# Query sketch of the first chunk in eight 32x64 matmuls, two v pieces on GpSimd's queue, larger weight loads

## The chip, the cores and the metric

The kernel runs on one core of one Trainium2 chip. The metric is the device time of one execution in microseconds (us), as a median of several runs. A core has five engines with instruction queues of their own: TensorE (PE in the profile, with PEld for its weight loads), VectorE (DVE), ScalarE (ACT), GpSimd (POOL) and SyncE (SP). Sixteen DMA engines move data; transfers are issued from SP's, ACT's or GpSimd's queue.

## What is computed

Polysketch attention over 4 batches, 4 heads, 1088 positions and head width 32, then a feed-forward layer with squared ReLU of width 2048, all in float32:

```python
def phi(x):
    a = np.einsum('rd,bhsd->bhsr', S1, x)      # r = 8
    b = np.einsum('rd,bhsd->bhsr', S2, x)
    return np.einsum('bhsi,bhsj->bhsij', a, b).reshape(*x.shape[:-1], 64)
q_p, k_p = phi(q), phi(k)
kv = np.einsum('bhsf,bhsd->bhfd', k_p, v)
z = np.sum(k_p, axis=2)
num = np.einsum('bhsf,bhfd->bhsd', q_p, kv)
den = np.einsum('bhsf,bhf->bhs', q_p, z)[..., None] + 1e-06
x = (num / den).transpose(0, 2, 1, 3).reshape(4352, 128)
h = np.maximum(x @ w_in, 0.0)                  # w_in 128 x 2048
out = (h * h) @ w_out                          # w_out 2048 x 128
```

## The kernel before

The 4352 tokens of x are cut into ten chunks of the feed-forward layer (256, 384, 448, 448, five of 512, 256 tokens). For each chunk PE multiplies by the 16 blocks of w_in (`ffn1`, L597, result in PSUM tile `pg`), ACT and DVE take the ReLU (`relu`, L607 and L609, tile `gt`) and the square (`square`, L620 and L622, tile `g`), and PE adds up the 16 blocks of w_out (`ffn2`, L641 and L636, tile `po`). A planner, the class `_Order`, lays the attention of later chunks and batches between these matmuls by costs and due times; it begins after the prologue and its inputs are not touched by the change.

The prologue (L221 to L847) is written out by hand, and its order of program text is the order on each engine. It makes x for the first 256 tokens:

- Loads (L221 to L229): S1 and S2; k of batch 0 in two pieces (columns 0 to 512, then the rest); the first 256 columns of q; v in eight pieces, four partition groups p of 32 rows by the ranges 0 to 4 and 4 to 9 of the nine k tiles. Piece (p = 0, 0 to 4) is issued from ACT's queue, all others from SP's.
- `keep_warm` gives PE bf16 matmuls of constants (L692), W0 = 5 ahead of the small matmul L703 that spreads S1 and S2 (tile `sp`, copied to `ss` by ACT at L706), and W1 = 3 after it.
- From L707 SP issues the rest: a second part of q, w_in in four pieces of 512 columns (256 KB each), w_out in four pieces of 256 KB, and the third part of q. The loads of the next batches follow on the same queue.
- `a_kT0` (DVE, L290) transposes k into `kt`; `a_qT` (DVE, L296) transposes q into `qT`.
- `a_kf` (L315) sketches k: for each tile of 128 positions, four matmuls with 32 stationary columns. ACT copies the second factor to `kb` (L321); `a_kp0` (DVE, L331) multiplies the factors into `kp`.
- `q0` (L756) sketches the first 256 columns of q into the four-bank PSUM tile `x0`. Its stationary operand `sq` holds S1's or S2's rows for two heads, with zeros where the heads do not match; GpSimd makes it from `ss` and the mask `own_q` (L721). ACT copies one factor to `qb0` (L767), and DVE multiplies the two into `qp0` (L774).
- `a_kv0` (L396) adds up kp times v and kp's sums over the nine tiles into `kvp`; its first matmul contracts all 128 partitions of v.
- The denominators (L816), the numerators (L821) and a few small steps give xT for the first 256 tokens (L844). `cast_wi` (GpSimd, L685) casts w_in in four pieces from `w_in32`. A matmul at L835 reads the first of them, and then `ffn1` begins.

PSUM tiles `pg` and `po` have two buffers each, `att` (four banks) has one.

Of the kernel before, what the change touches and what calls it, by code (L numbers as in the profile page):

```python
# [14 lines left out]
def _ap(t: bass.AP, p0: int, np_: int, off: int, free):  # L15
    p = list(t.ap)[0]
    return bass.AP(
        t.tensor, t.offset + p0 * p[0] + off, [[p[0], np_]] + [list(d) for d in free]
    )
# [88 lines left out]
def kernel(  # L108
# [11 lines left out]
    nc = tc.nc  # L120

    B, H, S, D = 4, 4, 1088, 32
# [5 lines left out]
    GT, G2, LA = 4, 6, 3.5  # L128
    LU = 4
    KC = [(0, 160), (160, 128)]  # L130
    W0, W1, W3 = 5, 3, 1
    ND, QT, WI, KL, QL = 2, 6.0, (1.0, 1.9), (30.0, 8.0), 4.0


# [10 lines left out]
    mult = mybir.AluOpType.mult  # L145
# [10 lines left out]
    psf = ctx.enter_context(tc.tile_pool(name="psf", bufs=2, space=bass.MemoryType.PSUM))  # L156
# [3 lines left out]
    def sb(name, cols, dt=F32, rows=128):  # L160
        return cpool.tile([rows, cols], dt, tag=name, name=name)
# [7 lines left out]
    kT, qT = sb("kT", SP), sb("qT", SP)  # L169
    xT = sb("xT", B * S + SP - S, F32R)  # L170
    w_in32, w_o, w_in = sb("w_in32", 2048), sb("w_o", 2048), sb("w_in", 2048, F32R)
    s_nat, ss, s2f = sb("s_nat", 32, rows=16), sb("ss", 80), sb("s2f", 32)
# [24 lines left out]
    def load_v(eng, b, p, t0=0, t1=NT):  # L197
        n = 32 * ((t1 if p < 3 else min(t1, NT - 2)) - t0)
        eng.dma_start(
            _ap(vn[b % 2], 32 * p, 32, 32 * t0, [[32 * NT, H], [1, n]]),  # L200
            bass.AP(
                v.tensor, v.offset + b * H * S * D + 32 * first(b, t0, p),
                [[G * D, 32], [S * D, H], [1, n]],
            ),
        )

    def load_wi(eng, c):
        eng.dma_start(
            w_in32[:, 512 * c : 512 * c + 512], moe_w_in[:, 512 * c : 512 * c + 512]
        )  # L210

    def load_wo(eng, c):
        eng.dma_start(
            _ap(w_o, 0, 128, 512 * c, [[128, 4], [1, 128]]),
            bass.AP(
                moe_w_out.tensor, moe_w_out.offset + c * 512 * 128,
                [[128, 128], [128 * 128, 4], [1, 128]],
            ),
        )

# [1 line left out]
    nc.sync.dma_start(s_nat[8:16, :], S2[:, :])  # L222
    load_k(nc.sync, 0, 0, 512)
    load_k(nc.sync, 0, 512, S)
    load_v(nc.scalar, 0, 0, 0, 4)
    load_q(nc.sync, 0, 0, 256)
    for t0, t1 in ((0, 4), (4, NT)):
        for p in range(0 if t0 else 1, 4):
            load_v(nc.sync, 0, p, t0, t1)  # L229

    zero_a = sb("zero_a", 8)
    nc.scalar.copy(zero_a[:, :], nc.const_aps.tensor(0.0, (128, 8), F32))

    sq, sel = sb("sq", 256), sb("sel", 320, rows=16)
    nc.vector.memset(sel[:, :], 0.0)
    nc.gpsimd.memset(_ap(vn[0], 96, 32, 32 * (NT - 2), [[32 * NT, H], [1, 64]]), 0.0)
    nc.gpsimd.memset(vn[0][:, VC : VC + 32], 1.0)
# [2 lines left out]
    kt0 = sb("kt0", SP)  # L240
# [8 lines left out]
    for i in range(2):  # L249
# [5 lines left out]
    own_h, own_q = sb("own_h", 4), sb("own_q", 2)  # L255
# [3 lines left out]
    nc.gpsimd.tensor_copy(  # L259
        _ap(sel, 0, 16, 64, [[80, 4], [1, 16]]), _ap(iden, 0, 16, 0, [[0, 4], [1, 16]])  # L260
    )
    nc.vector.tensor_reduce(
        out=own_h[:, :], in_=_ap(iden, 0, 128, 0, [[32, 4], [1, 32]]), op=add, axis=AX
    )
# [14 lines left out]
    def banks(t_, x, col, n, k=2):  # L279

        return _ap(t_, 0, 128, 512 * x + col, [[512, k], [1, n]])
# [5 lines left out]
    def a_kT0(t0, n):  # L287
        p = 3 if t0 + n > NT - 2 else 4
        i = 32 * (first(0, t0, 1) - first(0, t0, 0))
        nc.vector.transpose(  # L290
            _ap(kt0, 0, 128, 128 * t0, [[32, p], [128, n], [1, 32]]),
            _ap(kn[0], 0, 128, 32 * first(0, t0, 0), [[i, p], [32, n], [1, 32]]),
        )

    def a_qT(b, i0, n):
        nc.vector.transpose(qT[:, 32 * i0 : 32 * i0 + 32 * n], qn[b % 2][:, 32 * i0 : 32 * i0 + 32 * n])  # L296
# [10 lines left out]
                )  # L307


    def a_kf(t0, n, pool, tag):  # L310
        kf = pool.tile([128, 512], F32, tag=tag, name="kf")
        for t in range(n):
            for c in range(4):
                o = 128 * (t0 + t) + 32 * c
                nc.tensor.matmul(  # L315
                    _ap(kf, 32 * c, 32, 32 * t, [[32 * n, 2], [1, 32]]),
                    kt0[:, o : o + 32],
                    sf,
                )
        kb = wpool.tile([128, 32 * 3], F32, tag="kb", bufs=4, name="kb")  # L320
        nc.scalar.copy(kb[:, 0 : 32 * n], kf[:, 32 * n : 64 * n])  # L321
        st["kf", t0] = kf, kb

    def new_kp(b):

        st[b, "kp"] = wpool.tile([128, 64 * NT * H], F32, tag="kp", name="kp")

    def a_kp0(t0, n):

        kf, kb = st["kf", t0]  # L330
        nc.vector.tensor_tensor(  # L331
            out=_ap(st[0, "kp"], 0, 128, 256 * t0, [[64, 4 * n], [8, 8], [1, 8]]),
            in0=_ap(kf, 0, 128, 0, [[8, 4 * n], [1, 8], [0, 8]]),
            in1=_ap(kb, 0, 128, 0, [[8, 4 * n], [0, 8], [1, 8]]),
            op=mult,
        )
# [352 lines left out]
    def keep_warm(n, cols=512):  # L689
        t_ = st["warm"]  # L690
        for _ in range(n):
            nc.tensor.matmul(  # L692
                t_[:, 0:cols],
                nc.const_aps.tensor(1.0, (128, 128), mybir.dt.bfloat16),
                nc.const_aps.tensor(1.0, (128, cols), mybir.dt.bfloat16),
            )
# [8 lines left out]
        )  # L705
    nc.scalar.copy(ss[:, :], sp[:, 0:80])  # L706
    load_q(nc.sync, 0, 256, 640)  # L707
    load_wi(nc.sync, 0)
    load_wi(nc.sync, 1)
    load_wo(nc.sync, 0)  # L710
    load_wi(nc.sync, 2)
    load_wo(nc.sync, 1)
    load_wi(nc.sync, 3)
    for c in range(2, 4):
        load_wo(nc.sync, c)
    load_q(nc.sync, 0, 640, S)
    keep_warm(W1)
    a_kT0(0, 2)
    a_kT0(2, 2)
    for x in range(2):  # L720
        nc.gpsimd.tensor_tensor(  # L721
            out=_ap(sq, 0, 128, 128 * x, [[64, 2], [8, 8], [1, 8]]),
            in0=_ap(ss, 0, 128, 72 - 8 * x, [[0, 2]] + [[[0, 8], [1, 8]], [[1, 8], [0, 8]]][x]),
            in1=_ap(own_q, 0, 128, 0, [[1, 2], [0, 8], [0, 8]]),
            op=mult,
        )
    for h in range(H):
        nc.gpsimd.tensor_copy(
# [4 lines left out]
    for w in sw:  # L733
# [3 lines left out]
        out=_ap(sfk, 0, 128, 0, [[16, 2], [1, 16]]),  # L737
        in0=_ap(ss, 0, 128, 64, [[0, 2], [1, 16]]),
        in1=_ap(own_q, 0, 128, 0, [[1, 2], [0, 16]]),
        op=mult,  # L740
# [4 lines left out]

    a_kT0(4, 3)
    a_kT0(7, 2)
    a_qT(0, 0, 8)


    x0 = att("x0")

    def q0(x):
        for y in range(2):
            r, o = slice(64 * y, 64 * y + 64), 512 * (2 * x + y)
            nc.tensor.matmul(x0[:, o : o + 256], sq[r, 128 * x : 128 * x + 128], qT[r, 0:256])  # L756

    new_kp(0)
    qb0 = wpool.tile([128, 512], F32, tag="qb0", bufs=1, name="qb0")
    qp0 = wpool.tile([128, 512], F32, tag="qp0", bufs=1, name="qp0")  # L760
    a_kf(0, 2, psf, "po")
    a_kf(2, 2, psf, "pg")
    a_kf(4, 3, psf, "po")
    a_kf(7, 2, psf, "pg")
    q0(0)
    q0(1)
    nc.scalar.copy(_ap(qb0, 0, 128, 0, [[256, 2], [1, 256]]), banks(x0, 0, 0, 256))  # L767
    st[0, "kvp"] = psf.tile([128, 512], F32, tag="pg", name="kvp")
    for t0, n in ((0, 2), (2, 2), (4, 3), (7, 2)):
        a_kp0(t0, n)  # L770
        for t in range(t0, t0 + n):
            a_kv0(t)

# [388 lines left out]
```

## Time and profile before

| | us |
|---|---|
| median of 3 runs | 184.37 (184.09 to 184.5) |
| profiled execution | 184.44 |
| its span | 182.6 |
| granted TensorE clock | 0.998 |

| stretch, us | PE busy | DVE busy | ACT busy | POOL busy | DMA GB/s |
|---|---|---|---|---|---|
| 0 to 5 | 4.23 | 2.16 | 1.71 | 2.68 | 169 |
| 5 to 10 | 4.53 | 4.40 | 1.45 | 1.96 | 212 |
| 10 to 15 | 4.44 | 4.37 | 2.75 | 1.84 | 276 |
| 15 to 20 | 5.00 | 4.83 | 4.74 | 3.44 | 301 |
| 40 to 180 | 139.38 | 88.19 | 111.00 | 21.35 | 27 |

The span is the time from the first to the last instruction that the profile shows; the execution's own time has 1.84 us around it. Busy time is the time in which an engine has an instruction of the kind counted. Instruction groups are told by the line of the kernel, the engine, the operation and out<-in by tile names; x is a count. A float32 matmul is two instructions of PE.

### The profile page before, as it was taken

Reading aid. Unit: us, or ns where it says so; the run is one execution under the profiler, and the core shown is the slowest. Engines: PE = TensorE matmul, PEld = TensorE weight load, DVE = VectorE, ACT = ScalarE, POOL = GpSimd, SP = SyncE. Lnnn points to the kernel's source line nnn. Section 1 sums busy time; section 2 is a strip of 40 time slices with the busy share of each in tenths; the row PEclk is TensorE's granted clock in tenths of the full one; section 3 lists DMA queues with packets and bytes.
Section 4 is the critical chain, followed back from the end, with each engine's and each line's share of the span. In section 5 each row is a group of like instructions: output and inputs, shape, how many; then the busy total and the mean of one; then the engine's idle time right before and its main releaser. Section 6 shows DMA issues by size and latency. Waiting matters only on the chain.

```text
span 182.6 us, 3995 instructions
## 1 busy us (share of the span) xinstructions
PE 177.6 (97%) x1529; PEld 104.7 (57%) x1529; DVE 122.2 (67%) x262; ACT 136.0 (74%) x258; POOL 39.2 (21%) x158
## 2 busy tenths in 40 slices
PE   8899999999999999999999999999999999999992
PEld 2768876755645655555455554545555555555792
DVE  3979969999999961799994335996353334333640
ACT  3339679749948886799937778894777777777990
POOL 5535418438300002570018100500000000000000
PEclk9999999999999999999999999999999999999999
DMA  5899994010029500000030200003003000300111
GB/s 155 220 266 341 221 266 105 4 32 0 0 47 260 157 0 4 4 2 0 0 54 15 43 0 5 0 0 59 0 4 57 0 0 5 52 0 0 32 29 29
DMA packets 24610, 11.26 MB, mean 62 GB/s; under 512 B 17936, under 2 KB 23056, under 8 KB 24592
## 3 DMA queue, kind: packets, MB, share of 16 engines
q1 hardware_dynamic: 24272, 10.89, 24.5%
q8 instruction: 12, 0.20, 0.5%
q10 hardware_dynamic: 320, 0.13, 0.3%
q14 instruction: 6, 0.05, 0.1%
HBM read 8.78 MB, written 2.23 MB: 60 GB/s over the span
## 4 chain that ended last, share of the span: by engine, by line
PE 95%; DMA 2%; DVE 0%; SPq 0%; issue 0%; ACT 0%; ACTq 0%
PE po L641 61%; PE pg L597 18%; PE nd L550 3%; PE po L636 2%; PE pol L636 2%; DMA kn<-in_k_dram 2%; PE qc L303 2%; PE nd L414 1%; PE kvp L396 1%; PE qc L347 1%; PE kvp L414 1%; PE x L756 1%; PE kf L315 0%; PE nd L347 0%; DVE kt L290 0%
## 5 line engine op out<-in xcount | busy, mean ns | idle before, releaser
L641 PE MATMUL po<-g,w_o 128*128 128x512 f32 (+3 forms) x288 | 122.7, 547 | 0.2 <-PE pg L597 0.2
L609 ACT ACTIVATE gt<-pg 128x512 f32<-128x512 f32 (+3 forms) x144 | 75.2, 570 | 31.5 <-PE pg L597 31.0
L641 PEld LDWEIGHTS po<-g,w_o 128*128 128x128 f32 x288 | 53.4, 189 | 32.3 <-issue 24.8
L597 PE MATMUL pg<-xT,w_in 128*128 128x512 f32 (+3 forms) x160 | 70.2, 519 | 0.0
L620 ACT ACTIVATE g<-gt 128x512 f32<-128x512 f32 (+2 forms) x102 | 60.7, 623 | 1.6
L622 DVE TENSOR_TENSOR g<-gt 128x512 f32<-128x512 f32 (+3 forms) x43 | 30.4, 708 | 39.5 <-ACT gt L609 38.8
L597 PEld LDWEIGHTS pg<-xT,w_in 128*128 128x128 f32 x160 | 29.2, 190 | 28.5 <-ACT gt L609 11.6
L510 POOL COPY rd<-rc 32x9 f32<-32x9 f32 (+2 forms) x80 | 19.5, 243 | 26.4 <-DVE rc L502 23.2
L456 POOL COPY kv<-kvt 32x64 f32<-32x64 f32 x48 | 12.7, 264 | 44.7 <-DVE kvt L433 42.5
L519 DVE STREAM_SHUFFLE qa<-qc 128x576 f32<-128x576 f32 (+2 forms) x20 | 11.8, 646 | 0.0
L534 DVE TENSOR_TENSOR qp<-qa,qb 128x576 f32<-128x576 f32 (+2 forms) x20 | 10.8, 602 | 0.0
L482 DVE STREAM_TRANSPOSE qt<-qc 128x576 f32<-128x576 f32 (+2 forms) x10 | 5.8, 608 | 6.0 <-PE qc L347 4.3
L367 DVE TENSOR_TENSOR kp<-fs 128x576 f32<-128x576 f32 x12 | 8.7, 742 | 0.0
L645 DVE STREAM_TRANSPOSE oT<-po 128x512 f32<-128x512 f32 (+3 forms) x9 | 5.9, 651 | 2.1 <-PE po L641 2.1
L550 PE MATMUL nd<-qp,kv 32*32 32x288 f32 (+2 forms) x320 | 6.6, 354 | 0.0
L519 DVE STREAM_SHUFFLE qb<-qc 128x576 f32<-128x576 f32 (+2 forms) x10 | 6.1, 649 | 0.0
L567 DVE TENSOR_TENSOR xT<-nd,bc 128x576 fp32r<-128x576 f32 (+2 forms) x10 | 5.6, 589 | 0.6 <-PE nd L550 0.5
L636 PE MATMUL po<-w_o,g 128*128 128x128 f32 x32 | 5.8, 279 | 0.0
L296 DVE STREAM_TRANSPOSE qT<-qn 128x192 f32<-128x192 f32 (+3 forms) x11 | 5.7, 549 | 0.0
L636 PE MATMUL pol<-w_o,g 128*128 128x128 f32 x32 | 5.7, 275 | 0.0
L560 DVE STREAM_TRANSPOSE bc<-rd 128x576 f32<-128x576 f32 (+2 forms) x10 | 5.6, 593 | 0.0
L550 PEld LDWEIGHTS nd<-qp,kv 32*32 32x32 f32 x320 | 2.9, 103 | 3.6 <-issue 2.4
(106 smaller groups left out, 89.8 us busy)
## 6 DMA issues: line engine op xcount, KB each, us to landing
kn<-in_k_dram SPq DMA_DIRECT2D x3, 544.0 KB, 8.8
qn<-in_q_dram SPq DMA_DIRECT2D x3, 544.0 KB, 8.7
vn<-in_v_dram SPq DMA_DIRECT2D x9, 144.0 KB, 6.4
w_in<-in_moe_w_in_dram SPq DMA_DIRECT2D x4, 256.0 KB, 4.2
w_o<-in_moe_w_out_dram SPq DMA_DIRECT2D x4, 256.0 KB, 5.6
out_dram<-oT SPq DMA_DIRECT2D x12, 64.0 KB, 1.9
out_dram<-oT SPq DMA_DIRECT2D x8, 56.0 KB, 1.8
out_dram<-oT SPq DMA_DIRECT2D x8, 48.0 KB, 1.8
```

Of the source, the lines that this page charges most:

```text
L367: nc.vector.tensor_tensor(out=_ap(st[b, "kp"], 0, 128, 64 * NT * h, [[64, NT], [8, 8], [1, 8]]), in0=_ap(fs, 0, 128, o, [[32, NT], [1, 8], ...
L456: nc.gpsimd.tensor_copy(_ap(st[b, "kv"], 32 * c, 32, 64 * h, [[32, E], [1, 32]]), _ap(st["kvt"], 32 * h, 32, 0, [[64, E], [1, 32]]),)
L510: nc.gpsimd.tensor_copy(st[b, "rd", i0][32 * h : 32 * h + 32, n * c : n * c + n], st["rc"][32 * c : 32 * c + 32, n * h : n * h + n],)
L519: nc.vector.stream_shuffle(in_=banks(st[b, "qc", i0], 2 * x, 0, m), out=_ap(st[b, which, i0], 0, 128, 2 * m * x, [[m, 2], [1, m]]), mask=m ...
L534: nc.vector.tensor_tensor(out=st[b, "qp", i0, e][:, r], in0=st[b, f"qa{e}", i0][:, r], in1=st[b, "qb", i0][:, r], op=mult,)
L550: nc.tensor.matmul(nd[32 * h : 32 * h + 32, 512 * c : 512 * c + m], kv[r, o : o + 32], qp[r, m * h : m * h + m], start=(e == 0), stop=(e = ...
L597: nc.tensor.matmul(st["pg", u][:, n * i : n * i + n], w_in[:, 128 * (d0 + i) : 128 * (d0 + i) + 128], xT[:, c0 : c0 + n],)
L609: nc.scalar.activation(gt[:, 0:w], st["pg", u][:, 0:w], Relu)
L620: nc.scalar.activation(to, of, Square)
L622: nc.vector.tensor_tensor(out=to, in0=of, in1=of, op=mult)
L636: nc.tensor.matmul(po[x // 128][:, 0:128], g[:, x : x + 128], w, start=(d == 0), stop=(d == NB - 1),)
L641: nc.tensor.matmul(po[0][:, 0:n], w, g, start=(d == 0), stop=(d == NB - 1))
```

## The change

The sketch of q in the prologue becomes eight matmuls, one for each head and factor, with 32 contracted rows and 64 stationary columns; `sq` holds each factor once (128 columns in place of 256) and GpSimd makes it with two copies. The heads' results lie in halves of 64 partitions that are swapped for the first factor, so ACT copies `qb0` in two parts that swap them back. `a_kp0(0, 2)` is moved ahead of the transpose of q and of the later `a_kf`. The last `a_kf` group takes 64 stationary columns at a time.

The first two v pieces are issued from GpSimd's queue, behind the two copies into `sel`. w_in is loaded in two pieces of 512 KB, and w_out's second half in one of 512 KB. W1 is 2, and a warm-up matmul of 384 columns follows.

```diff
--- before.py
+++ after.py
@@ -128,7 +128,7 @@
     GT, G2, LA = 4, 6, 3.5
     LU = 4
     KC = [(0, 160), (160, 128)]
-    W0, W1, W3 = 5, 3, 1
+    W0, W1, W3 = 5, 2, 1
     ND, QT, WI, KL, QL = 2, 6.0, (1.0, 1.9), (30.0, 8.0), 4.0
 
 
@@ -204,17 +204,16 @@
             ),
         )
 
-    def load_wi(eng, c):
+    def load_wi(eng, c, n=1):
+        r = slice(512 * c, 512 * (c + n))
+        eng.dma_start(w_in32[:, r], moe_w_in[:, r])
+
+    def load_wo(eng, c, n=1):
         eng.dma_start(
-            w_in32[:, 512 * c : 512 * c + 512], moe_w_in[:, 512 * c : 512 * c + 512]
-        )
-
-    def load_wo(eng, c):
-        eng.dma_start(
-            _ap(w_o, 0, 128, 512 * c, [[128, 4], [1, 128]]),
+            _ap(w_o, 0, 128, 512 * c, [[128, 4 * n], [1, 128]]),
             bass.AP(
                 moe_w_out.tensor, moe_w_out.offset + c * 512 * 128,
-                [[128, 128], [128 * 128, 4], [1, 128]],
+                [[128, 128], [128 * 128, 4 * n], [1, 128]],
             ),
         )
 
@@ -222,16 +221,15 @@
     nc.sync.dma_start(s_nat[8:16, :], S2[:, :])
     load_k(nc.sync, 0, 0, 512)
     load_k(nc.sync, 0, 512, S)
-    load_v(nc.scalar, 0, 0, 0, 4)
     load_q(nc.sync, 0, 0, 256)
     for t0, t1 in ((0, 4), (4, NT)):
-        for p in range(0 if t0 else 1, 4):
+        for p in range(0 if t0 else 2, 4):
             load_v(nc.sync, 0, p, t0, t1)
 
     zero_a = sb("zero_a", 8)
     nc.scalar.copy(zero_a[:, :], nc.const_aps.tensor(0.0, (128, 8), F32))
 
-    sq, sel = sb("sq", 256), sb("sel", 320, rows=16)
+    sq, sel = sb("sq", 128), sb("sel", 320, rows=16)
     nc.vector.memset(sel[:, :], 0.0)
     nc.gpsimd.memset(_ap(vn[0], 96, 32, 32 * (NT - 2), [[32 * NT, H], [1, 64]]), 0.0)
     nc.gpsimd.memset(vn[0][:, VC : VC + 32], 1.0)
@@ -259,6 +257,8 @@
     nc.gpsimd.tensor_copy(
         _ap(sel, 0, 16, 64, [[80, 4], [1, 16]]), _ap(iden, 0, 16, 0, [[0, 4], [1, 16]])
     )
+    for p in range(2):
+        load_v(nc.gpsimd, 0, p, 0, 4)
     nc.vector.tensor_reduce(
         out=own_h[:, :], in_=_ap(iden, 0, 128, 0, [[32, 4], [1, 32]]), op=add, axis=AX
     )
@@ -307,14 +307,14 @@
                 )
 
 
-    def a_kf(t0, n, pool, tag):
+    def a_kf(t0, n, pool, tag, w=32):
         kf = pool.tile([128, 512], F32, tag=tag, name="kf")
         for t in range(n):
-            for c in range(4):
-                o = 128 * (t0 + t) + 32 * c
+            for c in range(0, 128, w):
+                o = 128 * (t0 + t) + c
                 nc.tensor.matmul(
-                    _ap(kf, 32 * c, 32, 32 * t, [[32 * n, 2], [1, 32]]),
-                    kt0[:, o : o + 32],
+                    _ap(kf, c, w, 32 * t, [[32 * n, 2], [1, 32]]),
+                    kt0[:, o : o + w],
                     sf,
                 )
         kb = wpool.tile([128, 32 * 3], F32, tag="kb", bufs=4, name="kb")
@@ -705,24 +705,20 @@
         )
     nc.scalar.copy(ss[:, :], sp[:, 0:80])
     load_q(nc.sync, 0, 256, 640)
-    load_wi(nc.sync, 0)
-    load_wi(nc.sync, 1)
+    load_wi(nc.sync, 0, 2)
     load_wo(nc.sync, 0)
-    load_wi(nc.sync, 2)
+    load_wi(nc.sync, 2, 2)
     load_wo(nc.sync, 1)
-    load_wi(nc.sync, 3)
-    for c in range(2, 4):
-        load_wo(nc.sync, c)
+    load_wo(nc.sync, 2, 2)
     load_q(nc.sync, 0, 640, S)
     keep_warm(W1)
+    keep_warm(1, 384)
     a_kT0(0, 2)
     a_kT0(2, 2)
     for x in range(2):
-        nc.gpsimd.tensor_tensor(
-            out=_ap(sq, 0, 128, 128 * x, [[64, 2], [8, 8], [1, 8]]),
-            in0=_ap(ss, 0, 128, 72 - 8 * x, [[0, 2]] + [[[0, 8], [1, 8]], [[1, 8], [0, 8]]][x]),
-            in1=_ap(own_q, 0, 128, 0, [[1, 2], [0, 8], [0, 8]]),
-            op=mult,
+        nc.gpsimd.tensor_copy(
+            _ap(sq, 0, 128, 64 * x, [[8, 8], [1, 8]]),
+            _ap(ss, 0, 128, 72 - 8 * x, [[[0, 8], [1, 8]], [[1, 8], [0, 8]]][x]),
         )
     for h in range(H):
         nc.gpsimd.tensor_copy(
@@ -745,29 +741,37 @@
 
     a_kT0(4, 3)
     a_kT0(7, 2)
-    a_qT(0, 0, 8)
 
 
     x0 = att("x0")
 
     def q0(x):
-        for y in range(2):
-            r, o = slice(64 * y, 64 * y + 64), 512 * (2 * x + y)
-            nc.tensor.matmul(x0[:, o : o + 256], sq[r, 128 * x : 128 * x + 128], qT[r, 0:256])
-
-    new_kp(0)
+        for h in range(H):
+            r, o, p = slice(32 * h, 32 * h + 32), 512 * (2 * x + h // 2), 64 * ((h + 1 - x) % 2)
+            nc.tensor.matmul(
+                x0[p : p + 64, o : o + 256], sq[r, 64 * x : 64 * x + 64], qT[r, 0:256]
+            )
+
     qb0 = wpool.tile([128, 512], F32, tag="qb0", bufs=1, name="qb0")
     qp0 = wpool.tile([128, 512], F32, tag="qp0", bufs=1, name="qp0")
+    new_kp(0)
     a_kf(0, 2, psf, "po")
+    a_kp0(0, 2)
+    a_qT(0, 0, 8)
     a_kf(2, 2, psf, "pg")
     a_kf(4, 3, psf, "po")
-    a_kf(7, 2, psf, "pg")
+    a_kf(7, 2, psf, "pg", 64)
     q0(0)
     q0(1)
-    nc.scalar.copy(_ap(qb0, 0, 128, 0, [[256, 2], [1, 256]]), banks(x0, 0, 0, 256))
+    for i in range(2):
+        nc.scalar.copy(
+            _ap(qb0, 64 * i, 64, 0, [[256, 2], [1, 256]]),
+            _ap(x0, 64 - 64 * i, 64, 0, [[512, 2], [1, 256]]),
+        )
     st[0, "kvp"] = psf.tile([128, 512], F32, tag="pg", name="kvp")
     for t0, n in ((0, 2), (2, 2), (4, 3), (7, 2)):
-        a_kp0(t0, n)
+        if t0:
+            a_kp0(t0, n)
         for t in range(t0, t0 + n):
             a_kv0(t)
```

## The prediction

> **What bounds the kernel now.** I read the page's busy shares first, then the chain of waits over the first 20 us, where all the edits lie. The lines are the span, the engines, and the chain (start, length, what).
>
> ```profile
> span 182.6 us, 3995 instructions
> PE 177.6 (97%) x1529; PEld 104.7 (57%) x1529; DVE 122.2 (67%) x262; ACT 136.0 (74%) x258; POOL 39.2 (21%) x158
> ...
> 1.62 3.52 DMA kn<-in_k_dram
> 5.14 0.02 issue
> 5.16 0.59 DVE kt L290
> 5.75 0.14 issue
> 5.89 0.77 PE kf L315 x40
> 6.66 1.06 PE x L756 x8
> 7.72 2.25 PE kvp L396 x72
> ...
> 12.37 0.42 PE warm L835
> 12.80 0.54 PE pg L597 x4
> 13.34 0.38 PE qc L303 x29
> 13.71 0.48 PE pg L597 x2
> 14.20 0.21 issue
> 14.41 0.67 PE po L641 x2
> ```
>
> PE is 97% busy, and from 14.4 us on it hardly waits: a gain is worth its full size only where PE waits before that. It waits for the second piece of k (landed 5.14), then runs kf, the query sketch q0 (tile x, L756, 1.06 us) and kvp without a gap, so an earlier start of kvp is an earlier everything up to L597. There is one more hole: 0.21 us before the first L641. The timeline (start, length, instruction) shows what fills it and how DVE is ordered around q0.
>
> ```profile
> 5.93 0.40 DVE L296 STREAM_TRANSPOSE qT<-qn 128x256 f32<-128x256 f32 x1
> 6.25 0.65 DVE L331 TENSOR_TENSOR kp<-kf,kb 128x512 f32<-128x512 f32 x1
> ...
> 13.42 0.61 POOL L685 CAST w_in<-w_in 128x512 fp32r<-128x512 f32 x1 [1.64 <-DMA w_in<-in_moe_w_in_dram]
> 13.48 0.82 DVE L622 TENSOR_TENSOR g<-gt 128x256 f32<-128x256 f32 x1
> 14.23 0.41 DVE L622 TENSOR_TENSOR g<-gt 128x256 f32<-128x256 f32 x1
> ```
>
> The same DVE square took 0.82 us beside GpSimd's third cast of w_in and 0.41 us after it. The first one feeds the matmul at 14.41, so the hole is this collision; undisturbed the square would end at 13.89, and PE would be free at 14.20.
>
> **The change, part by part.**
>
> *q0's matmuls.* A 128x256 f32 matmul alone takes 0.43 us (two instructions; L641's pairs). Before, four such with 64 rows took 1.06: two at a time, 0.86, plus 0.20 for the group's start and drain. After, there are eight with 32 rows and 64 columns, and the eight (row group, column half) places are all different. L303 shows that such places work at once along rows and columns: 16 matmuls of 96 columns, 0.16 us each, took 0.44 (13.27 to 13.71), where even four in turn per row group would need 0.64. So q0 costs 0.43 + 0.20 = 0.63 us; the bounds are 0.43 (no start cost) and 1.06 (only rows overlap).
>
> *q0's start.* a_kp0(0, 2) now stands ahead of the transpose of q on DVE. By the rows, DVE does kt at 5.16 and 5.67, then kp from 5.93 for 0.58 (start to start, 6.25 to 6.83), then qT from 6.51 to 6.91. q0 starts 0.14 after that (the lag from kt to kf): 7.05 instead of 6.66, less whatever k lands earlier. It ends at 7.05 + 0.63 = 7.68 against 7.72. So the two edits together bring only 0.04 us. The new wait on DVE, kp0(0, 2) for kb, has qT and the rest of kp behind it and costs nothing: kb is there at 5.24 + 0.21 = 5.45. The rest of kp ends as before (same DVE work), 0.3 us or more ahead of PE's need of each group (the last at 8.97, needed at 9.47).
>
> *kf's last group in 64-column pieces.* It is 8 instructions in place of 16, at 19 ns each (0.77 us for 40), 0.15 us at most; PE waits for qT then, so it is worth 0. Without that cover it would be worth its 0.15.
>
> *The warm-up* loses 128 of 1536 columns, 0.12 us at L692's 0.46 per 512. kf's start is at 4.75, with kt at 4.58 and the warm-up's end at 4.81; what follows waits for k's second piece. Worth 0.
>
> *v pieces.* Piece 0 leaves ACT's queue (issue 1.38 us, in front of k's second piece in the transfers), and piece 1 leaves SP's; both go onto GpSimd's queue behind the sel copies, which end at 2.34. The gain is on k: 65.5 KB less ahead of it at the 335 to 391 GB/s of 3.0 to 4.5 us is 0.17 to 0.20 us; at the 205 GB/s just before, 0.32. If GpSimd's transfers come among k's, it is 0. I take 0.17, since k's issues end at 2.06 and GpSimd's begin after 2.34. No GpSimd DMA is in this trace. Its issue is between 0.34 us (ACT's) and 1.40 (the longest issue, L208); I take 0.61, the length of GpSimd's cast, the nearest row of that engine on a large tile. With 3.3 us to landing (a v piece on SP, by the list of DMA issues), piece 1 lands at 2.34 + 1.22 + 3.3 = 6.86, needed at 7.51: hidden, by 0.65 us. Behind the issues wait sq, irep, sw and sfk; sq (0.80 us before, two copies of 0.25 to 0.40 now) would be ready by 3.56 + 0.8 = 4.4, or 5.9 at the dearest issue, needed at 6.9. ACT's freed 0.34 us lies ahead of its copy at 3.55, which waits for PE: 0.
>
> The Trainium skill's page DMA: Bandwidth & Descriptors, section Anatomy of one DMA — SWDGE (gpsimd) path, gives a fixed cost of about 2.0 us plus bytes by 436 GB/s to a GpSimd transfer. By that estimate two in turn would land by 2.34 + 2 x 2.15 = 6.64 us, and the sum stays as it is; no run here shows it yet.
>
> *Copies of q0.* ACT now takes two copies of 64 partitions in place of one of 128 (0.59). At the same 0.59 each they end at 7.6 + 1.18 = 8.8, when DVE comes to qp (8.89 less 0.17); qp then ends near 9.5, and its reader, den at L816, starts at about 10.1. Worth 0, with 0.5 us of cover.
>
> *Weight loads.* SP drops one v issue (3.31/7 = 0.47 us) and three weight issues (0.43 each). w_in's first half is issued at 5.92 and lands between 5.92 + 4.2 = 10.1 and the 11.1 of its second piece before; the first cast is over by 11.7 at the latest, needed at L835 at 12.16. That is hidden. The second half lands as one. It is 256 KB more than what landed at 13.42, 0.8 to 1.2 us at 303 to 208 GB/s, and is issued 0.47 + 0.43 = 0.90 sooner: 13.42 + 0.8 - 0.90 = 13.3 if the whole lead carries, 13.42 + 1.2 = 14.6 if none does. I take 13.9, the middle. Then the DVE square, which starts at 13.48 - 0.21 = 13.27 and ends at 13.68, meets no cast, and the hole closes: 0.21. The casts at 13.9 to 15.1 lie beside the second square, qt and pd; pd was slowed before too (0.68 us beside the fourth cast, 0.25 later), and POOL and DVE have gained the 0.41 already. PE needs the third cast at 15.31; it is over at 14.5 (15.2 at the worst). w_o's pieces land in the bytes' order, some 15 to 17 us; its d 8 is read after 20.
>
> **Sum:** 0.04 + 0.17 + 0.21 = 0.42 us. The profiled execution took 184.44 us with its 182.6 us span (1.84 around it), 0.07 above the median; 184.37 - 0.42 = 183.95, told as **183.9**.
>
> **Rivals.**
>
> *The collision stays* (w_in's second half lands at 13.3 to 13.5): the square is slowed as before, and only 0.21 is left: 184.16. For it: SP reaches the load sooner. Against: the load is twice as long.
>
> *The cast comes late.* If the second half lands where its last piece did before (15.19), the cast ends at 15.8 and PE waits at L597 from 15.31: all the gain is lost, 184.4. Against it: one load of w_o less is ahead.
>
> *Slower: GpSimd's v pieces gate kvp.* All 128 partitions of v are contracted in kvp's first matmul, so the later piece holds back all of PE. Landing is 2.34 + 2p + 3.3 for an issue of p. From p = 0.9 it costs, from 1.1 it eats the 0.42. At p = 1.40 kvp starts at 8.54 in place of 7.72; with the hole's 0.21 returned, +0.6: 185.0. For it: the issue is unknown and both go through one engine; against it: 0.65 us of slack.
>
> *Slower: q0's row groups get in each other's way.* Heads 0 and 1 (and 2 and 3) now write one PSUM bank from two row groups; L756, L303 and L550 before give each row group its own bank, so the trace does not show this. If two such matmuls take turns and starts are in order, q0 is five turns of 0.43 plus 0.20 = 2.35 us, kvp starts at 9.23, 1.5 us late, and with the hole closed the time is 185.7; if all turns pair up, q0 is 1.06 again and the time 184.4. For plain overlap: they write different partition halves, and L303's four column tiles share a bank at once.
> The Trainium skill, TensorEngine Tiling, Restrictions and Gotchas, says that different row tiles cannot access the same PSUM bank simultaneously. By that rule the 185.7 is the time; the trace neither bears it out nor denies it.
>
> **How the numbers follow.** About 0.2% (0.37 us) is what a measurement of this kernel can tell from no change. Forecast 0.50 (its own range 183.5 to 184.15: bounds of k's gain 0 to 0.32, q0 0.43 to 0.63 and the hole); collision stays 0.14; late cast 0.08; v late 0.16; bank turns 0.12. Faster: 0.46 of the forecast and 0.04 of the collision, 0.50. Slower: 0.13 of v late, 0.12 of bank turns, 0.02 of late cast, 0.27. The same: the rest, 0.23. The range 183.4 to 185.0 leaves out the bank turns (0.12), the dearest v (0.04) and some 0.04 below.
>
> **What would show it.** Right: k's second piece lands near 4.97; q0 runs about 0.6 us from 6.9; kvp starts at 7.5, right after it; the first square takes 0.41 and no hole stands before L641. Wrong: kvp with a wait for v; q0 of over 1 us; a wait of L597 for a cast; a DVE chain to nd (19.2) that comes no earlier, so that PE waits there instead.

## The result, and the profile after

The changed kernel takes 185.17 us (median of 19 runs, 184.6 to 189.64) against 184.46 us (19 runs, 184.09 to 185.77) for the kernel before beside it: a ratio of 1.0042, 95% interval 1.0024 to 1.006. A repetition gave 1.0027 (1.001 to 1.0044). It is slower by 0.5 to 0.8 us, where 0.42 us of gain was forecast. The profiled execution took 185.28 us. Ratios, here and below, leave out executions more than 1.5% above the fastest of the same kernel (here 188.16 and 189.64 us); medians do not.

First the page of the changed kernel: span, engines, and GpSimd's own DMA queue, which is new.

```profile
span 183.5 us, 3995 instructions
PE 178.0 (97%) x1529; PEld 104.9 (57%) x1529; DVE 121.9 (66%) x262; ACT 136.5 (74%) x259; POOL 40.2 (22%) x160
...
q0 software_dynamic: 64, 0.13, 0.2%
```

The chain of waits of the changed kernel from 2 to 17 us (start, length, what):

```profile
2.10 4.19 DMA qn<-in_q_dram
6.29 0.02 issue
6.31 5.93 DMA w_in<-in_moe_w_in_dram
12.24 0.05 issue
12.29 0.62 POOL w_in L685
12.91 0.04 issue
12.95 0.50 PE warm L839
13.45 0.47 PE pg L597 x4
13.93 0.38 PE qc L303 x29
14.30 0.47 PE pg L597 x2
14.77 0.48 PE po L641 x2
15.26 0.24 PE pg L597 x2
15.49 0.43 PE po L641 x2
15.93 0.49 PE pg L597 x2
16.42 0.86 PE po L641 x4
```

The chain no longer goes through k, the sketches and kvp. It goes through q's first part, the first half of w_in and its cast. The 512 KB load lands at 12.24, 5.93 us after its issue, and L839 (L835 before) starts at 12.95 where the chain before has it at 12.37. The hole ahead of the first L641 is gone: L597 runs into it at 14.77. The timeline of the same execution (start, length, instruction, and in brackets the idle time before it with what ended it) shows the steps one by one:

```profile
2.30 1.26 POOL L199 DMA_DIRECT2D vn<-in_v_dram  x2
4.92 0.84 DVE L290 STREAM_TRANSPOSE kt<-kn 128x384 f32<-128x384 f32 x2 [0.26 <-DMA kn<-in_k_dram]
...
5.69 0.68 DVE L331 TENSOR_TENSOR kp<-kf,kb 128x512 f32<-128x512 f32 x1
...
6.32 0.45 DVE L296 STREAM_TRANSPOSE qT<-qn 128x256 f32<-128x256 f32 x1
...
6.91 0.69 PE L751 MATMUL x<-qT,sq 32*64 32x256 f32 x16
...
7.53 2.32 PE L396 MATMUL kvp<-vn,kp 128*64 128x64 f32 x72
...
12.95 0.50 PE L839 MATMUL warm<-w_in 128*128 128x512 f32 x1 [0.70 <-POOL w_in L685]
...
14.07 0.75 DVE L622 TENSOR_TENSOR g<-gt 128x256 f32<-128x256 f32 x2
...
15.25 1.20 POOL L685 CAST w_in<-w_in 128x512 fp32r<-128x512 f32 x2 [1.79 <-DMA w_in<-in_moe_w_in_dram]
```

Up to kvp all went as forecast, only smaller: kvp starts at 7.53, 0.12 us before the 7.65 that the timeline before gives it. Then PE waits 0.70 us for the cast. The next lines of the chain of the kernel before, behind its first L641 (14.41), show what comes after that:

```profile
15.08 0.23 PE pg L597 x2
15.31 0.43 PE po L641 x2
15.74 0.24 PE pg L597 x2
15.98 0.86 PE po L641 x4
```

At the two L597 ahead of the first L641 the changed kernel is 0.59 us late (14.30 against 13.71). The closed hole takes most of that back: at the end of the first pair of L641 it is 0.18 late (15.26 against 15.08). Then the third cast of w_in, the first one of the second half, starts only at 15.25, the pair of L597 behind it takes 0.49 in place of 0.24, and the chain is 0.44 late (16.42 against 15.98). So both halves of w_in come late in this execution, and the second one costs some 0.26 us. At the denominators L550 the chain is 0.45 late (19.72 against 19.27). From there to PE's last matmul the two chains are the same, shifted by 0.45 to 0.46 us: the last copy, `obl` on DVE, starts at 179.87 against 179.41.

That is half of the 0.84 us between the two profiled executions. The other half comes after the last copy. The next lines are the instructions that close the program (durations in ns min/median/max, then the start in us of the first and last), of the kernel before:

```profile
L1157 SPq EVENT_SEMAPHORE  x7: 17/28/558, 180.3 to 182.6; - x7
...
L1157 SPq DRAIN  x3: 7/7/7, 181.9 to 182.2; - x3
...
L1157 POOLq EVENT_SEMAPHORE_RANGE_CLEAR  x1: 98/98/98, 182.3 to 182.3; - x1
```

and of the changed kernel:

```profile
L1161 SPq EVENT_SEMAPHORE  x8: 17/28/28, 182.3 to 183.4; - x8
...
L1161 SPq DRAIN  x3: 7/7/7, 182.7 to 183.0; - x3
...
L1161 POOLq EVENT_SEMAPHORE_RANGE_CLEAR  x1: 139/139/139, 183.1 to 183.1; - x1
```

Before, SP's semaphore instructions begin at 180.3, while the last output transfers are under way, and one of them (558 ns) waits inside that time; SP's drain follows at 181.9, 2.47 us after the start of the last copy. After, the first of them ends its wait only at 182.3, all the others still stand behind it, and the drain is at 182.7, 2.80 us after the copy. The two records, SP alone, with the start counted from the last copy and the semaphores that each instruction looks at (the two output transfers issued last use 100 and 110 before, and 106 and 105 after):

```
before                    after
0.91  105, 104            2.41  105, 103
0.98  107, 103            2.48  106, 100
1.59  108, 100            2.55  107, 112
2.18  109, 102            2.61  108, 111
2.41  110, 106            2.68  109, 102
2.47  drain               2.74  110, 104
                          2.80  drain
3.23  end of the span     3.63  end of the span
```

SP looks at the semaphores two at a time, 105 first and 110 last in both records, 0.065 us each time. The issue records show why the place of the wait moved: all transfers that SP and ACT issue take eight semaphores in rotation, and GpSimd's take two of their own (111, 112). Before there are 89 such transfers and the one that lands last has the semaphore that is looked at last. After there are 84 (two v pieces went to GpSimd, three weight loads were joined), so the rotation ends five places earlier, and five looks are left to do after the landing: 5 x 0.065 = 0.33 us. GpSimd's clearing and what surrounds it takes 0.83 in place of 0.76. Together 0.40 us, with no engine doing any work for it.

### The profile page after: what moved, and what is told of

Its sections match the earlier page's. It is cut to its first block, busy times and chain, and to the rows that moved or that the text cites. A ratio compares the mean times of both kernels' runs of the same rounds, so it can differ in the third digit from the quotient of the medians.

```text
span 183.5 us, 3995 instructions
## 1 busy us (share of the span) xinstructions
PE 178.0 (97%) x1529; PEld 104.9 (57%) x1529; DVE 121.9 (66%) x262; ACT 136.5 (74%) x259; POOL 40.2 (22%) x160
## 4 chain that ended last, share of the span: by engine, by line
PE 91%; DMA 6%; SPq 1%; POOL 0%; issue 0%; DVE 0%
PE po L641 60%; PE pg L597 18%; PE nd L550 3%; DMA w_in<-in_moe_w_in_dram 3%; DMA qn<-in_q_dram 2%; PE po L636 2%; PE pol L636 2%; PE qc L303 2%; PE nd L414 1%; PE qc L347 1%; PE kvp L414 1%; SPq L181 0%; PE nd L347 0%; POOL w_in L685 0%; PE warm L839 0%; SPq L221 0%
## 5 line engine op out<-in xcount | busy, mean ns | idle before, releaser
L641 PE MATMUL po<-g,w_o 128*128 128x512 f32 (+3 forms) x288 | 122.7, 546 | 0.0
L641 PEld LDWEIGHTS po<-g,w_o 128*128 128x128 f32 x288 | 53.4, 189 | 31.9 <-issue 24.8
L597 PE MATMUL pg<-xT,w_in 128*128 128x512 f32 (+3 forms) x160 | 70.2, 519 | 0.0
L597 PEld LDWEIGHTS pg<-xT,w_in 128*128 128x128 f32 x160 | 29.2, 190 | 28.6 <-ACT gt L609 11.5
L550 PE MATMUL nd<-qp,kv 32*32 32x288 f32 (+2 forms) x320 | 6.6, 354 | 0.0
L550 PEld LDWEIGHTS nd<-qp,kv 32*32 32x32 f32 x320 | 2.9, 103 | 3.6 <-issue 2.4
```

The source lines that it names most:

```text
L550: nc.tensor.matmul(nd[32 * h : 32 * h + 32, 512 * c : 512 * c + m], kv[r, o : o + 32], qp[r, m * h : m * h + m], start=(e == 0), stop=(e = ...
L597: nc.tensor.matmul(st["pg", u][:, n * i : n * i + n], w_in[:, 128 * (d0 + i) : 128 * (d0 + i) + 128], xT[:, c0 : c0 + n],)
L641: nc.tensor.matmul(po[0][:, 0:n], w, g, start=(d == 0), stop=(d == NB - 1))
```

## The experiments

In short: Q is the query sketch with the warm-up, kf and kp0 edits, V the two v pieces on GpSimd's queue, W the larger weight loads. The theories on record before each run are mostly about the landing of loads. None of them has the end of the program in it; that was read in the traces of these runs afterwards. The ratio of each run is to the kernel before on the same chip; "cast" is the start of the first cast of w_in in the one profile that each label has.

**One part undone, or alone.** W undone, in the changed kernel:

```diff
-    load_wi(nc.sync, 0, 2)
+    load_wi(nc.sync, 0)
+    load_wi(nc.sync, 1)
     load_wo(nc.sync, 0)
-    load_wi(nc.sync, 2, 2)
+    load_wi(nc.sync, 2)
     load_wo(nc.sync, 1)
-    load_wo(nc.sync, 2, 2)
+    load_wi(nc.sync, 3)
+    for c in range(2, 4):
+        load_wo(nc.sync, c)
```

> The changed kernel with the weight loads as before (eight of 256 KB). Theory W (the 512 KB load of w_in holds back the first cast): the first cast starts at 10.4 to 11.2 us, L839 follows the chain at about 12.25, time 184.0 to 184.3. Theory V (GpSimd's v pieces make everything on SP's queue land later): the first cast is still late, time 184.9 or more. Theory N (the three engines' order in the prologue): as V.

Measured: 1.0000 (0.9979 to 1.0022), 184.48 us. The timeline of this kernel at the casts:

```profile
10.65 0.61 POOL L685 CAST w_in<-w_in 128x512 fp32r<-128x512 f32 x1 [3.82 <-DMA w_in<-in_moe_w_in_dram]
11.97 0.62 POOL L685 CAST w_in<-w_in 128x512 fp32r<-128x512 f32 x1 [0.71 <-DMA w_in<-in_moe_w_in_dram]
...
12.19 0.50 PE L842 MATMUL warm<-w_in 128*128 128x512 f32 x1
```

The first 256 KB are there at 10.65, the second at 11.97, and L842 needs only the first cast: no wait. The 0.70 us goes with the larger loads.

The same edit the other way round, W alone in the kernel before:

> The kernel before with only the weight loads changed (w_in in two, w_out's second half in one). Theory W: the first cast waits for 512 KB, starts at 11.5 to 12.3 us, PE waits for it at the matmul that reads the first cast, time 184.7 to 185.3. Theory V: no change, 184.3 to 184.6.

Measured: 1.0005 (0.9986 to 1.0025), 184.80 us; cast at 11.11, no wait of PE. In this profile the large load alone isn't late enough to matter.

V undone, in the changed kernel (Q and W stay):

```diff
+    load_v(nc.scalar, 0, 0, 0, 4)
     load_q(nc.sync, 0, 0, 256)
...
-        for p in range(0 if t0 else 2, 4):
+        for p in range(0 if t0 else 1, 4):
...
-    for p in range(2):
-        load_v(nc.gpsimd, 0, p, 0, 4)
```

> The changed kernel with v's first two pieces back on ACT's and SP's queues; q sketch and weight loads stay changed. Theory W: still slow, 184.8 to 185.3. Theory V: q and v land as before, the first cast by 11.5, time 184.0 to 184.4.

> The changed kernel with v's pieces back on ACT's and SP's queues once more. If the larger loads alone carry the loss and the first result was luck: 184.9 or more, the first cast at 11.7 us or later. If the v pieces on a second queue are needed for it: 184.4 to 184.7, the first cast by 11.6 again.

Measured: 1.0007 (0.9986 to 1.0028) and 1.0004 (0.9986 to 1.0022), casts at 11.09 and 10.73. Without V the large load is in time in both profiles, and no loss is left that can be told from none.

V alone in the kernel before, and V with W without Q:

> The kernel before with only v's first two pieces on GpSimd's queue. Theory E (GpSimd's pieces make the loads behind them land later, and that costs only where a 512 KB load must land whole): the casts keep their slack, 184.3 to 184.7. Theory V (GpSimd's queue costs by itself): 184.9 or more.

> The kernel before with both load changes, v by GpSimd and the larger weight loads, and q's sketch as before. Theory E: both together are what costs, first cast at about 12.2 us, 184.9 to 185.4. If the q sketch's part is needed for the loss: 184.3 to 184.7.

Measured: V alone 1.0009 (0.9989 to 1.0029); V with W 1.0032 (1.0009 to 1.0054), 185.03 us. The pair costs what the whole change costs, so Q is not what loses. The profile of V with W was one of its best executions (184.55 us, cast at 11.25, no wait). Its PE stream is 0.41 us faster than before (last copy at 179.00), and yet the execution is 0.11 us slower than before's: the end costs 0.40 us, and about 0.13 more lies outside the span.

Q alone:

> The kernel before with only the q sketch part (eight matmuls, kp0 ahead of qT, 64 columns in the last kf group, shorter warm-up). By the forecast's steps kvp starts 0.04 us sooner and nothing else moves: 184.3 to 184.5. If the swapped halves or the new order cost more than shown, 184.6 or more.

Measured: 0.9988 (0.997 to 1.0006), 184.48 us. Nothing that can be told from no change, at best a small gain.

**Which half, and which load.** The first half of w_in in two loads of 256 KB, all else as changed, run twice:

```diff
-    load_wi(nc.sync, 0, 2)
+    load_wi(nc.sync, 0)
+    load_wi(nc.sync, 1)
```

> The changed kernel with only the first 512 KB load of w_in split in two of 256 KB; the second half stays one load. Theory W and V together (the load is late because of GpSimd's pieces, and it costs only because one 512 KB load must land whole before the first cast): the first cast starts near 10.7, PE does not wait for it; a wait of up to 0.4 us for the second half's cast at L597 may stay: 184.3 to 184.7. If the merged second half costs most: 184.9.

> The changed kernel with the first 512 KB load split once more. If the first half is what costs: 184.4 to 184.7 again and the first cast by 11.1 us. If it was luck: 184.9 or more.

Measured: 1.0012 (0.9997 to 1.0027) and 1.002 (0.9988 to 1.0052); cast at 10.72 in both, L840 without a wait. The second half in two loads instead:

> The changed kernel with only w_in's second half in two loads; the first half stays one load of 512 KB. If the first half carries the loss: as the changed kernel, 184.9 or more. If the second half carries it: as with the first half split, 184.4 to 184.7.

Measured: 1.0025 (1.0005 to 1.0045), 184.90 us. Its profile is of an execution of 188.37 us: the first 512 KB landed at 14.28, and PE waited 2.6 us for the cast. It is the longest such landing seen. The intervals of the two splits overlap each other and that of the changed kernel, so the times alone don't say which half costs more.

Q, with the first half in two loads, the second half in one, w_out's second half in one, and no V:

> q sketch as changed, v on ACT's and SP's queues as before, w_in's first half in two loads, its second half and w_out's second half in one each. All casts in time, the third one clear of the first square: kvp starts as in the kernel before, the hole before the first L641 is closed: 184.0 to 184.2. If the larger loads cost by themselves: 184.4 or more.

Measured: 1.0024 (1.0006 to 1.0042), 185.07 us. Here it is the second half that comes late; timeline, and PE's waits (total us, times, longest):

```profile
15.48 1.17 POOL L684 CAST w_in<-w_in 128x512 fp32r<-128x512 f32 x2 [2.59 <-DMA w_in<-in_moe_w_in_dram]
```

```profile
PE pg L596 <- POOL w_in L684: 0.7, 1, 0.7
```

So each half can hold back PE when it is one load, in some executions. This execution also has 2.42 us outside its span, where the kernel before has 1.79; why isn't known.

Q with all of w_in in one load of 1 MB, no V:

```diff
-    load_wi(nc.sync, 0, 2)
+    load_wi(nc.sync, 0, 4)
     load_wo(nc.sync, 0)
-    load_wi(nc.sync, 2, 2)
     load_wo(nc.sync, 1)
     load_wo(nc.sync, 2, 2)
```

> q sketch as changed, v as before, and w_in in one load of 1 MB (a larger dose of the suspected cost, without GpSimd's queue). Theory W: the first cast waits for the whole megabyte, 12.6 us or later (its bytes are through at about 12.0 by the traffic so far), PE waits at the matmul that reads the first cast, and the granted clock may drop behind the wait: 184.9 to 187. If only GpSimd's queue costs: 184.3 to 184.6.

Measured: 1.005 (1.0019 to 1.0082), 185.58 us; cast at 13.15. In the profiled execution PE was late on its own account (kvp at 8.63; the trace's clock records begin only at 9.87, and the last section says what PE does before them), so the cast held nothing back there, and the profile can't say which of the two cost the time.

**Why V delays the load.** GpSimd's pieces moved to other partitions (p = 0 and 2 in place of 0 and 1), for the theory that 64 neighbouring partitions load some DMA engines more than others:

```diff
-    for p in range(2):
+    for p in (0, 2):
         load_v(nc.gpsimd, 0, p, 0, 4)
...
-        for p in range(0 if t0 else 2, 4):
+        for p in (range(4) if t0 else (1, 3)):
```

> The changed kernel, but GpSimd's two v pieces are those of partitions 0 to 31 and 64 to 95 (the changed kernel: 0 to 31 and 32 to 63); SP takes the other two. Theory S (GpSimd's pieces load some DMA engines more than others, by partition, and the w_in load lands with the slowest): with the two pieces on different engines q's first part lands some 0.3 us sooner (3.9 us after its issue in place of 4.2), w_in's first half by 11.7, time 184.3 to 184.7. Theory Q (any bytes on GpSimd's queue push SP's back): as the changed kernel, w_in's first half at about 12.2, 184.9 or more.

Measured: 1.009 (1.0057 to 1.0122), 186.53 us: worse, not better, so the theory in that form fell. Which partitions the pieces fill may still matter. Its timeline, and then its stretches (busy us and counts of PE, PEld, DVE, ACT, POOL; granted clock; DMA share and GB/s):

```profile
12.60 1.17 POOL L685 CAST w_in<-w_in 128x512 fp32r<-128x512 f32 x2 [5.76 <-DMA w_in<-in_moe_w_in_dram]
...
13.26 0.71 PE L839 MATMUL warm<-w_in 128*128 128x512 f32 x1 [0.89 <-POOL w_in L685]
13.77 1.05 PE L597 MATMUL pg<-xT,w_in 128*128 128x256 f32 x4
```

```profile
10.00:12.00 2.00, 1.66 (x28) 1.01 (x32) 1.80 (x8) 0.43 (x2) 0.00 (x0) 1.00 0.90 275
12.00:14.00 2.00, 1.11 (x11) 0.82 (x12) 0.71 (x2) 0.37 (x1) 1.17 (x2) 0.85 1.06 357
14.00:16.00 2.00, 2.00 (x39) 1.50 (x39) 1.57 (x3) 1.49 (x3) 1.36 (x2) 0.50 1.12 378
16.00:18.00 2.00, 2.00 (x11) 1.74 (x11) 1.83 (x10) 1.50 (x4) 0.21 (x2) 0.80 1.11 302
```

The wait for the cast was 0.89 us here, 0.19 more than in the changed kernel's profile, and then the granted clock fell to 0.50 in the stretch 14 to 16 and was back at 1.00 in 18 to 20. The four L597 matmuls took 1.05 us in place of 0.63. So the late load was paid twice in this execution.

One v piece on GpSimd's queue instead of two, and both pieces on ACT's queue instead of GpSimd's:

> The changed kernel with one v piece on GpSimd's queue in place of two; the other goes back to SP's queue, ahead of the others. If GpSimd's bytes are what delays SP's transfers, half of the delay is left: w_in's first half lands at about 11.7 (11.1 without, 12.2 with two), q's first part 3.9 us after its issue, time 184.4 to 184.8. If it is the engine that issues and not the bytes, nothing changes: 184.9 or more.

> The changed kernel with v's first two pieces on ACT's queue, issued at about 2.9 and 3.4 us, in place of GpSimd's. If it is GpSimd's own way of issuing that makes SP's loads late: as with v back on the old queues, 184.4 to 184.8. If any second queue with two pieces beside SP's does it: as the changed kernel, 184.9 or more. The copy of ss on ACT is some 0.2 us later in both.

Measured: one piece 1.003 (1.0001 to 1.0058), cast at 11.40; on ACT's queue 1.0049 (1.0029 to 1.0068), 185.34 us, cast at 11.66. ACT issued the two pieces at 1.44 and 1.82 us, not at the 2.9 and 3.4 that were expected, so this run differs from V undone mainly in the second piece, which SP issues at 2.56 there. The delay isn't particular to GpSimd's way of issuing. Over all profiles with a first load of 512 KB, the cast starts at 11.25 to 12.60 (14.33 once) where v comes on a second queue (from GpSimd, or both pieces from ACT), and at 10.73 to 11.11 where it doesn't (one piece from ACT at 1.37 to 1.38 us, the rest from SP). The issue isn't later for it (6.31 and 6.26 in the changed kernel's two profiles, 6.38 and 6.39 with V undone); the load takes longer to land, 5.9 and 5.5 us against 4.7 and 4.3. Each of these loads is recorded as sixteen landings, and it isn't all of them that come later. In the changed kernel's two profiles the first eleven and twelve are in by 10.19 and 10.37 us, and the others come at 11.01 to 12.24 and 11.20 to 11.73; with V undone all sixteen come at 9.58 to 11.04 and 9.88 to 10.68. So a few stragglers hold back the first cast.

**Edits within Q.** Without the matmul on w_in whose result nothing reads (W3 = 0), and with q's transpose back ahead of kp0(0, 2), both with Q alone:

> Only the q sketch part of the change, and the matmul between the attention of the first chunk and the first L597 (the one that reads the first cast and whose result nobody uses) left out. The chain gives it 0.42 us, of which xT's end hides all but 0.13: 184.1 to 184.3. If that matmul is what keeps the clock up: above 184.8.

> Only the q sketch part, with the transpose of q ahead of kp0(0, 2) on DVE as in the kernel before. The forecast's term says that the new order costs 0.58 us of q0's start and eats all that the eight matmuls save; without it q0 starts when kf ends (6.6 to 6.7), ends 0.45 us sooner, and kvp ends about 0.2 sooner (then DVE's kp bounds it): 184.0 to 184.3, the first version faster than the kernel before. If the order has nothing to do with it: 184.3 to 184.5.

Measured: 1.0000 (0.9975 to 1.0026) and 0.9994 (0.9985 to 1.0003). Neither matters: with the order turned, q0 starts at 6.77 and kvp then waits for kp, until 7.59.

**The changed kernel again:**

> The changed kernel once more, for a second profile of the first cast and beside the three others on one chip. If the late first load is the cause and not that one execution: the first half of w_in lands at 11.6 us or later again, PE waits at the matmul that reads it, 184.9 to 185.5.

Measured: 1.0027 (1.001 to 1.0044), 185.11 us (184.24 to 188.7). In this profile the first half landed in 5.5 us, the cast started at 11.79 and L839 at 12.45, some 0.1 us of wait. PE's stream was 0.14 us faster than before (last copy at 179.27), and the execution at 184.69 was 0.25 us slower.

**The end of the program in all twenty profiles.** "End" is the time from the start of the last copy to SP's drain plus the time from the drain to the end of the span, less the 2.47 + 0.76 us of before. "Rest" is the measured ratio less 1, times 184.46, less that end.

| kernel | transfers of SP and ACT | copy to drain | drain to end | end, us | ratio | rest, us |
|---|---|---|---|---|---|---|
| before | 89 | 2.47 | 0.76 | 0 | 1 | 0 |
| Q; Q without W3; Q, qT first | 89 | 2.47, 2.47, 2.48 | 0.76 | 0 | 0.9988, 1.0000, 0.9994 | -0.22, 0, -0.11 |
| Q+V; V | 87 | 2.60, 2.60 | 0.83 | 0.20 | 1.0000, 1.0009 | -0.20, -0.03 |
| Q, second half and w_out joined | 87 | 2.60 | 0.76 | 0.13 | 1.0024 | +0.31 |
| W; Q+W twice | 86 | 2.67, 2.66, 2.66 | 0.76 | 0.19 | 1.0005, 1.0007, 1.0004 | -0.10, -0.06, -0.12 |
| changed, v on ACT | 86 | 2.66 | 0.76 | 0.19 | 1.0049 | +0.71 |
| Q, w_in in one load | 85 | 2.74 | 0.76 | 0.27 | 1.005 | +0.65 |
| changed, first half split, twice | 85 | 2.73, 2.73 | 0.83 | 0.33 | 1.0012, 1.002 | -0.11, +0.04 |
| changed, second half split; one piece on GpSimd | 85 | 2.72, 2.72 | 0.83 | 0.32 | 1.0025, 1.003 | +0.14, +0.23 |
| V+W | 84 | 2.80 | 0.83 | 0.40 | 1.0032 | +0.19 |
| changed, twice | 84 | 2.80, 2.81 | 0.83 | 0.40 | 1.0042, 1.0027 | +0.37, +0.10 |
| changed, p = 0 and 2 | 84 | 2.81 | 0.83 | 0.40 | 1.009 | +1.26 |

The copy-to-drain time is 2.47 us plus 0.065 us for each transfer fewer than 89, to 0.01 us, in every one of the twenty profiles, whatever else differs. In each of them the look that meets the last landing stands at 2.40 to 2.42 us after the copy's start, and what differs is how many looks are left: 0, 2, 3, 4 and 5 at 89, 87, 86, 85 and 84 transfers. With GpSimd's queue in use 0.07 us come on top. The end is the same in each profile of one kind, unlike the landings in the prologue. A ratio's interval is about 0.3 to 0.5 us to either side, so single rests are weak; as a group they divide. They lie near or below zero where the first cast needs only 256 KB, or where W is there without a second queue for v. They are positive where 512 KB must land first and v comes on a second queue, where all of w_in is one load, and where the second half was seen late. No kernel was made that varies the number of transfers alone, say by padding the rotation back to its turn of eight; that wasn't tried.

No version beat the kernel before by more than the measurement can tell: the best is Q alone.

## Why the prediction was wrong, point by point

The sum was wrong in its sign. The mechanisms that it named for the gain are nearly all there; two costs were not in it.

- **k earlier, 0.17.** Right: k's second piece started its transposes at 4.92 in place of 5.16, 0.24 us sooner.
- **q0, 0.63.** Right: 0.69 us busy, and kvp starts 0.62 after q0 does. Two row groups wrote one PSUM bank at once in different partition halves, so the bank rival (2.35 us) fell. The Trainium skill's rule in TensorEngine Tiling (Array Packing), Restrictions and Gotchas, that row tiles cannot access one bank simultaneously, did not hold in this form: serial turns would have taken more than three times the 0.69.
- **q0's start, 7.05 less 0.17.** Right: 6.91. Yet kvp came only 0.12 earlier, not 0.04 + 0.17 = 0.21. Of the 0.09 that is missing, 0.06 is q0 (0.69 us in place of 0.63) and 0.03 its start. kp0(0, 2) started at 5.69, even sooner than the 5.93 - 0.17 of the sum, but qT came 0.63 behind it in place of 0.58 (q's first part had landed only at 6.29) and q0 0.59 behind qT in place of 0.54.
- **GpSimd's v pieces.** The cover held: 0.63 us an issue where 0.61 was taken, and kvp never waited for v. The landing was 3.7 to 3.8 us after the issue. The estimate of 2.15 us for it, worked out from the Trainium skill's page DMA: Bandwidth & Descriptors, section Anatomy of one DMA — SWDGE (gpsimd) path, is too short here.
- **Copies of q0.** Right: 1.17 us for the two, and qp began at 8.90, inside its cover.
- **The hole before L641, 0.21.** Right in its mechanism, too small in its size: two squares in 0.75 us in place of 1.16, no hole, and 0.41 us of lag taken back (0.59 to 0.18, by the chains above). It isn't owed to the larger loads alone: with Q alone the first square takes 0.42 us too, in all three profiles, and with W alone it takes 0.82, with casts at 13.07 and 13.63. What counts is where the third cast happens to fall.
- **The first half of w_in, "That is hidden."** This step failed. It was said to be issued at 5.92, to land by 11.1 at the latest and to be cast by 11.7. It was issued at 6.31, landed at 12.24 and was cast at 12.91, and L839 waited 0.70 us. Two things were wrong in it. SP had to wait with the issue: in the rotation of eight semaphores w_in's first load waits for a v piece before (semaphore 109), and for q's first part after (semaphore 107), since V took two transfers out of the rotation; and q's part landed only at 6.29. So the load went out 0.09 us sooner than before (6.40), not 0.48. And the load took 5.93 us to land: the bounds 10.1 to 11.1 came from one execution's landings of 256 KB pieces. Over the profiles of these runs, first casts after a 256 KB load start at 9.72 to 11.09 and after a 512 KB load at 10.73 to 12.60, with 14.33 once. In the profile before, L835 started at 12.30, and the cast must be done by then, so a 512 KB load is hidden in some executions and not in others. The rival of the late cast was named for the second half alone, at 0.08. That half came late too: forecast for 13.9 and at worst 14.6, it was cast from 15.25 on, and the two L597 behind it took 0.49 us in place of 0.24, which is 0.26 of the chain's lag; in the repetition (cast at 13.92) nothing waited for it; in the Q variant with w_in's second half joined PE waited 0.7 us for it.
- **"SP drops one v issue and three weight issues": a term put at nothing.** This step failed too, and it is the surer loss. The sum uses these issues for the lead of w_in alone and takes everything after PE's last matmul as fixed, without a reason. What lies outside the span did stay (1.78 us against 1.79). The end inside the span did not: five transfers fewer on SP and ACT put SP's last looks behind the last landing, 0.33 us, and GpSimd's queue adds 0.07. This 0.40 us alone uses up the forecast's 0.42.

With both in place the numbers close for the profiled pair: kvp -0.12, the wait for the first half +0.70, the hole -0.41, the second half +0.26, which is +0.45 for the stream to the rounding; end +0.40; outside the span -0.01: the 0.84 measured. What is shown: the end cost, by its steps of 0.065 us over twenty profiles; that the first half is waited for, by the profile, and that the wait goes with W undone, with the first half split and with V undone, by theirs. The sizes in the medians are less sure, as their intervals overlap. What is open: why the last landings of the large load come later when v comes on a second queue; how often it is late over many executions, since each kernel run has one profile; and what the start of the full clock, which differs from execution to execution (see the end), adds to the scatter of the prologue.

## What to carry to other kernels

Joining loads saves issues on a queue, but a consumer of the first part then waits for the last byte: ask when the first instruction that reads it needs it, and give the landing a spread from several executions, not the one of a single trace. Removing or moving transfers shifts which semaphore every later transfer gets, and with it which earlier load an issue must wait for and how much bookkeeping stands behind the last landing; compare the records after the last matmul before trusting a difference of 0.2%.

## What the runs showed of the hardware

- The end of the program is not constant: SP looks at the semaphores two at a time, 0.065 us each look, and what is left after the last landing ranged from none to five looks over the twenty profiles.
- A wait of PE of 0.70 us in the changed kernel's profile left the granted clock at 1.00; one of 0.89 us, with GpSimd's pieces on other partitions, was followed by a stretch at 0.50, and in that execution the last copy started 1.40 us later (181.27 against 179.87). A wait of 2.6 us, with the second half split, was followed by 0.50 as well (stretch 16 to 18); one of 0.7 us in the Q variant with the second half joined was not.
- The f32 matmuls of kf (L315) started 14 ns apart in the profile before and 27 ns apart in the changed kernel's. The trace's clock records begin at 4.60 us in the first and at 6.48 in the second; a page prints 1.00 also where there is no record yet. Wherever kf runs across the start of the first record, its step changes from 27 to 14 ns within 0.3 us of it. That start differs between executions of one kernel (4.65 and 7.09 us with the first half split); over all profiles it lies at 3.97 to 7.22 us, and once at 9.87.
- Of the sixteen landings of the first 512 KB, the last came 2.7 us after the first in the changed kernel's profile (9.51 to 12.24) and 1.5 us after it with V undone (9.58 to 11.04).
